# Output projection of a recurrent attention loop: column halves in two PSUM banks, the last three blocks in two passes

## The chip, the cores and the metric

The kernel runs on one core of one Trainium2 chip. The metric is the time of one execution on the device in microseconds (us), lower is better. A profile is one further execution, taken by the hardware profiler.

## The reference

Two independent parts write the two halves of the output's columns. Part B is a state-space convolution over 2048 steps, which the change does not touch. Part A is attention over 64 segments of 32 rows, where 8 memory rows of each segment's result become part of the next one's input:

```python
for s in range(n_seg):                       # 2048 / 32 = 64 segments
    xs = x[:, s * seg_len:(s + 1) * seg_len, :].copy()
    h = jnp.concatenate([mem, xs], axis=1)   # 8 + 32 rows of 1024
    q = jnp.einsum('btd,dhe->bhte', h, Wq)   # 32 heads of 128; k and v likewise
    ...
    scores = jnp.einsum('bhqe,bhke->bhqk', q, k) * scale
    scores = jnp.where(mask[None, None], scores, -1000000000.0)
    p = _softmax(scores, axis=-1)
    o = jnp.einsum('bhqk,bhke->bhqe', p, v)
    o = jnp.einsum('bhte,hed->btd', o, Wo)   # the output projection
    mem = o[:, :M, :].copy()                 # 8 rows go into the next segment
    outs.append(o[:, M:, :])
```

So segment s + 1 cannot start its projections before the first rows of segment s's output projection are known.

## The kernel before

Part B runs first; while it runs, the work of part A that doesn't depend on the memory is done (keys, queries and values of the last 8 rows of each segment, "left rows", go to DRAM as PKd and VXd). Then `part_a` loops over the 64 segments, with 32 rows (8 memory rows and 24 others) in `hT`. Schedule and order are written out by hand: each engine executes its instructions in the order of the code, and the framework inserts the waits.

*Weights.* The four weight matrices are cut in blocks of 128 x 2048. Most blocks stay in SBUF for the whole loop. Thirteen blocks a segment are streamed from DRAM (512 KB each) through five slots (`wst`) on SP's queue, in the order of use: k 2 and 3, q 2, k 1 and 5, q 4, v 2 and 7, v 4 and 7, and blocks 4, 8 and 13 of the output projection. A load is issued when the block five places ahead in that order has been used. Block 7 of q and k and block 15 of the output projection are held in PSUM and copied into SBUF when they are due, by DVE: `fetch` (L337), for block 15 two copies into the arena (`Oa`, `Ob`) and one into `S`.

*One segment.* The projections (`quads`, L416) multiply hT, 32 columns wide, with a block in four matmuls of 512 columns that run side by side in four column tiles of TensorE. Then come transposes (L427), scores (L441, L444), the softmax on DVE and ACT, and the value products (`pv_x`, L497 and L501) for two groups of 16 heads, with results o0 and o1 in SBUF. `pv_l` is the value product of the left rows.

*The output projection* (`oproj`, L529) goes through 16 blocks of two heads each. For each head, four matmuls of 256 columns in four column tiles add into a 128 x 256 area of one PSUM bank, `pp[:, 1, :]`: column tile qt holds result columns 256 qt to 256 qt + 255. The blocks run 0 to 4 (from o0), then the second value product, then 5 to 7, then 8, 10, 12, 14, 9, 11, 13, 15 (from o1).

*The end of a segment*, in TensorE's order: `pv_l`; two transposes (L631) of the two 128-column halves of the result; the next segment's first `quads`. Between them: DVE copies the first half of `pp[:, 1, :]` into SBUF (L625), ACT the second (L625), and after the transposes DVE copies the memory rows of each into `hT` (L633):

```python
for j in range(2):
    (nc.scalar.copy if j else nc.vector.tensor_copy)(out=osb[:, 128 * j:128 * j + 128], in_=pp[:, 1, 128 * j:128 * j + 128])
pl = ps.tile([128, 4, 32], F32, name="pl", tag="b2")
pv_l(pl[:], 1, V1, L1)
```

Behind that ACT copies the left rows' results (L636, L639), issues the load of the next PKd and the store to RSd. PSUM banks are named by tags: `b0` to `b3` are used in turn, `keep0` to `keep3` hold the kept blocks. Before the change, both value products are in `b1`, `pp` (the left rows of the first group beside the projection's result) is in `b3`, `pl` in `b2`, and the transposes go to `b0` and `b1`.

After the loop the left rows' output projection runs (L669).

Of the kernel before, what the change touches and what calls it, by code (L numbers as in the profile page):

```python
# [10 lines left out]
BF16 = mybir.dt.bfloat16  # L11
F32 = mybir.dt.float32
# [252 lines left out]
def load_resident(tc, pool, src, key, W_res, eng=None, t_=None):  # L265
    if t_ is None:
        t_ = pool.tile([128, 2048], BF16, name="W_%s" % "_".join(str(i) for i in key))
    (eng or tc.nc.sync).dma_start(out=t_[:].rearrange("e (h d) -> e h d", h=2) if key[0] == "o" else t_[:], in_=src(key))
    W_res[key] = t_


def part_a(ctx, tc, x, src, WD, HE, seg_len, out_a, ahead, W_res, rest, places, first):
    nc = tc.nc
    S, Dm = x.shape
    M = 8
    SL = seg_len
    E = 128
    KC = Dm // 128
    NS = S // SL
    assert SL == 32 and M == 8 and Dm == 1024 and HE == 4096  # L280
    XM = 24
# [5 lines left out]
    ident, mask, BD, BDx, BDL, hT = ahead.consts  # L287
# [14 lines left out]
    def unit(key):  # L302
        if key in rest:

            rest.remove(key)
            load_resident(tc, wres, src, key, W_res, None, places.pop(0)() if places else None)
        if key in W_res:
            return W_res[key]
        if key in KEPT:
            return ahead_of.pop(key) + halves.get(key, [])  # L310
        between.pop(key, lambda: None)()
        if key in first:
            return first.pop(key)
        if key[0] == "v":
            for k_ in rest[0:3 if key[1] == 0 else 1]:
                rest.remove(k_)
                load_resident(tc, wres, src, k_, W_res, None, outs.pop(0) if outs else None)
        return stage(key, WD[key][:])
# [3 lines left out]
    ps = ctx_l.enter_context(tc.tile_pool(name="a_ps", bufs=1, space=PSUM))  # L322
# [16 lines left out]
    def stage(key, in_):  # L339
        t_ = wst.tile([128, 2048], BF16, name="wst", tag="w%d" % (loads[0] % SLOTS))  # L340
        loads[0] += 1
        nc.sync.dma_start(out=t_[:].rearrange("e (h d) -> e h d", h=2) if len(in_.shape) == 3 else t_[:], in_=in_)
        return t_
# [26 lines left out]
    def columns(w, lo, n):  # L370

        if not isinstance(w, list):
            return [(0, w[:, lo:lo + n])]
        return [(max(lo, l_) - lo, t_[:, max(lo, l_) - l_:min(lo + n, l_ + n_) - l_]) for l_, n_, t_ in w if l_ < lo + n and lo < l_ + n_]

    def load_pk(j):
        pk = at("pk", 512)
        nc.scalar.dma_start(out=pk, in_=PKd[j])
        return pk
# [28 lines left out]
    for s in range(NS):  # L408
        def quads(m, t, kcs, a=None):
            if a is None:  # L410
                a = ps.tile([128, 512], F32, name="acc", tag=BANK[m, t])
            for kc in kcs:
                w = unit((m, t, kc))
                for g in range(4):
                    for o_, rhs in columns(w, 512 * g, 512):
                        nc.tensor.matmul(a[32 * g:32 * g + 32, o_:o_ + rhs.shape[1]], lhsT=hT[:, kc, :], rhs=rhs,  # L416
                                         start=(kc == 0), stop=(kc == KC - 1), tile_position=(0, 32 * g), skip_group_check=True)
            return a

        def evac(a, name):  # L420
            q = at(name, 512)
            nc.scalar.copy(out=q, in_=a[:])  # L422
            return q
# [35 lines left out]
        def powers(sc, i):  # L459
            nc.scalar.activation(out=flat(sc, i), in_=flat(sc, i), func=ACT.Exp, scale=scale)  # L460

        def weigh(sc, i, pn):
            x, m_ = flat(sc, i), maxima(i)
            nc.vector.tensor_reduce(out=m_, in_=x, axis=AX.X, op=ALU.add)  # L464
            nc.vector.reciprocal(out=m_, in_=m_)
            pn = at(pn, x.shape[1], NK)
            nc.vector.tensor_tensor(out=pn, in0=x, in1=bc(m_.unsqueeze(2), [128, x.shape[1], NK]), op=ALU.mult)
            return pn

        def turn(pn, pt):  # L470
            n = pn.shape[1]
            pt = at(pt, n + n // 4, SL)
            nc.vector.transpose(out=pt[:, 0:n, :], in_=pn[:, :, 0:SL])
            nc.vector.transpose(out=pt[:, n:n + n // 4, :], in_=pn[:, :, SL:NK])  # L474
            return pt
# [19 lines left out]
        def pv(p, t, V, pb, lbs):  # L495
            for hl in range(4):
                nc.tensor.matmul(p[:, hl, :], lhsT=V[:, 128 * hl:128 * hl + 128], rhs=pb[:, hl, :],  # L497
                                 start=(hl == 0), stop=False, skip_group_check=True)
            p, lo = p.rearrange("p a b -> p (a b)"), 0
            for lb in lbs:  # L500
                nc.tensor.matmul(p[:, lo:lo + lb.shape[1]], lhsT=vl[:, t, :], rhs=lb,  # L501
                                 start=False, stop=True, skip_group_check=True)
                lo += lb.shape[1]

        def pv_x(t, V, pb, lbs):

            p = ps.tile([128, 4, 128], F32, name="pv", tag="b1")
            pv(p[:], t, V, pb.rearrange("p a b c -> p a (b c)"), lbs)
            return p

        def evac_o(p, name, parts=1):
            o, n = at(name, 4, 4, SL), 4 // parts
            for i in range(0, 4, n):
                copy = nc.vector.tensor_copy if i + n < 4 else nc.scalar.copy
                copy(out=o[:, i:i + n], in_=p[:, i:i + n, :].rearrange("p a (g q) -> p a g q", g=4))
            return o

        def pv_l(pl, t, V, L):

            pv(pl, t, V, L[:, 0].rearrange("p (a b) k -> p a (b k)", a=4), [L[:, 1].rearrange("p a k -> p (a k)")])  # L520

        def oproj(po, us, oT):
            for u in us:
                w = unit(("o", u))
                for hh in range(2):
                    h = 2 * u + hh
                    for qt in range(4):
                        for o_, rhs in columns(w, 1024 * hh + 256 * qt, 256):
                            nc.tensor.matmul(po[32 * qt:32 * qt + 32, o_:o_ + rhs.shape[1]], lhsT=oT[:, h % 4, (h % 16) // 4, :], rhs=rhs,  # L529
                                             start=False, stop=(h == 31), tile_position=(0, 32 * qt), skip_group_check=True)  # L530

        a = quads("k", 0, (0, 2, 4, 6, 1, 3, 5, 7))
        k0 = evac(a, "k0")
# [2 lines left out]
        a = quads("q", 0, range(0, 6))  # L536
# [4 lines left out]
        a = quads("k", 1, range(0, 3))  # L541
# [16 lines left out]
        a = quads("q", 1, range(KC))  # L558
# [3 lines left out]
        a = quads("v", 0, range(0, 4))  # L562
# [34 lines left out]
        a = quads("v", 1, range(0, 5))  # L597
        vl = vx[:, 0:256].rearrange("p (t e) -> p t e", t=2)
        pv0 = pv_x(0, V0, pb0, lb0)
        pp = ps.tile([128, 2, 256], F32, name="pp", tag="b3")  # L600
        pv_l(pp[:, 0, 0:128].rearrange("p (a k) -> p a k", a=4), 0, V0, L0)
        o0 = evac_o(pv0, "o0")
# [6 lines left out]
        V1 = evac(a, "V1")  # L609
        if s + 1 < NS:  # L610
            put_xt(vx)
        below(sc1, 1)
        powers(sc1, 1)
        oproj(pp[:, 1, :], range(0, 5), o0)
        pv1 = pv_x(1, V1, pb1, [lb1])
        o1 = evac_o(pv1, "o1", 2)
        lt1 = turn(weigh(sc1, 1, "ln1"), "lt1")
        oproj(pp[:, 1, :], range(5, 8), o0)
        L1 = left_blocks(lt1, 0, "L1")
        fetch(("o", 15))  # L620
        oproj(pp[:, 1, :], (8, 10, 12, 14, 9, 11, 13, 15), o1)
        ob = at("ob", 2, 256)
        osb = ob[:, 0, :]
        for j in range(2):
            (nc.scalar.copy if j else nc.vector.tensor_copy)(out=osb[:, 128 * j:128 * j + 128], in_=pp[:, 1, 128 * j:128 * j + 128])  # L625
        pl = ps.tile([128, 4, 32], F32, name="pl", tag="b2")
        pv_l(pl[:], 1, V1, L1)
        if s + 1 < NS:
            pt_o = [ps.tile([128, 4, SL], BF16, name="tro", tag=tag) for tag in ("b0", "b1")]
            for j in range(2):  # L630
                nc.tensor.transpose(out=pt_o[j][:].rearrange("p a b -> p (a b)"), in_=osb[:, 128 * j:128 * j + 128], identity=ident[:])  # L631
            for j in range(2):
                nc.vector.tensor_copy(out=hT[:, :, XM:SL].rearrange("p (q j) r -> p j q r", j=2)[:, j], in_=pt_o[j][:, :, XM:SL])  # L633
        if s + 1 < NS:
            fetch(("k", 0, 7))
        nc.scalar.copy(out=ob[:, 1, 0:128], in_=pp[:, 0, 0:128])  # L636
        if s + 1 < NS:
            pk = load_pk(s + 1)
        nc.scalar.copy(out=ob[:, 1, 128:256], in_=pl[:].rearrange("p a k -> p (a k)"))  # L639
        if s + 1 < NS:  # L640
            stores(s, ob)

# [1 line left out]
    wo = {}  # L644
# [17 lines left out]
    for b in range(4):  # L662
        pe = [ps_k.tile([128, 512], F32, name="pe", tag="keep%d" % (2 * (b % 2) + n)) for n in range(2)]
        for u in order:
            for hh in range(2):
                h = 2 * u + hh
                hi = 16 * (h // 16) + 4 * (h % 4) + (h % 16) // 4
                for n in range(2):
                    nc.tensor.matmul(pe[n][:], lhsT=left[2 * b + hi // 16][:, 128 * (hi % 16):128 * (hi % 16) + 128],  # L669
                                     rhs=wo[u][:, 1024 * hh + 512 * n:1024 * hh + 512 * n + 512], start=(u == order[0] and hh == 0),  # L670
                                     stop=(u == order[-1] and hh == 1))
# [1120 lines left out]
```

## Time and profile before

| | |
|---|---|
| Runs | 1873.58, 1884.78, 1887.85 us; median 1884.78 |
| Profiled execution | 1869.79 us, span 1868.1 us, mean granted clock 0.982 |
| Loop of part A | about 640 to 1840 us of the span |
| TensorE (PE) | 1763.2 us busy, 94% of the span, 31563 matmuls |
| VectorE (DVE) | 1344.2 us, 72% |
| ScalarE (ACT) | 924.7 us, 50% |
| Output projection (L529), all 64 segments | groups of 108.6, 92.8 us and smaller ones |
| DMA | 627.78 MB, mean 336 GB/s |

How to read it: a matmul's time in the profile is from its start to its modelled end, and matmuls overlap, so that counts and starts say more than busy times. PE stands for matmuls, PEld for weight loads, POOL for GpSimd, SP for the queue that issues the weight loads. In a row of the timeline the columns are start, length of the whole group, engine, line, operation, output and input tile, shape, count and, in brackets, the idle time before it with what ended it. The DMA share is the mean busy share of the core's 16 DMA engines.

### The profile page before, as it was taken

The page shows a single profiled execution, that of the slowest core. Times are in us where ns is not written, and L with a number is a line of the kernel's source. Part 1 is how long each engine was busy: PE and PEld are TensorE (multiplying, and loading weights), DVE is VectorE, ACT ScalarE, POOL GpSimd, SP SyncE. Part 2 cuts the span into 40 slices and gives each one's busy share as a digit, 9 for nine tenths or more (in the row PEclk, how much of TensorE's full clock was granted, in tenths as well). Part 3 has the DMA queues.
Part 4 walks back from the last instruction along what each step waited for, and adds up shares of the span by engine and source line. Part 5 has one row for each costly group of instructions (what it writes and reads, how often), then busy time and mean ns, then how long its engine had stood idle before and what let it go on. Part 6 is the DMA issues. An engine that isn't in the chain of part 4 may idle for free.

```text
span 1868.1 us, 73881 instructions
## 1 busy us (share of the span) xinstructions
PE 1763.2 (94%) x31563; PEld 1083.0 (58%) x31563; DVE 1344.2 (72%) x3367; ACT 924.7 (50%) x1663; POOL 518.9 (28%) x908
## 2 busy tenths in 40 slices
PE   8999999877986999999999999999999999999999
PEld 3666665556773655555555555555655555555554
DVE  8599989889992666676767676666766676767650
ACT  8799999881112444444444444444443444444430
POOL 2355454437871111111111111111111111211130
PEclk8999999989997999999999999999999999999999
DMA  8889999678889999999999999999999999999993
GB/s 225 248 247 265 269 264 272 194 217 283 265 299 366 375 391 376 378 380 384 385 390 388 384 389 387 377 381 388 389 384 384 371 387 380 384 383 378 383 367 87
DMA packets 350961, 627.78 MB, mean 336 GB/s; under 512 B 95124, under 2 KB 217500, under 8 KB 348584
## 3 DMA queue, kind: packets, MB, share of 16 engines
q1 hardware_dynamic: 307160, 568.55, 85.3%
q10 hardware_dynamic: 36816, 29.59, 4.8%
q0 software_dynamic: 6656, 24.92, 3.6%
q8 instruction: 247, 4.05, 0.9%
q14 instruction: 82, 0.67, 0.1%
HBM read 565.48 MB, written 72.16 MB: 341 GB/s over the span
## 4 chain that ended last, share of the span: by engine, by line
PE 64%; DVE 14%; DMA 12%; ACT 4%; issue 3%; POOL 2%; SPq 0%; DVEq 0%; POOLq 0%; ACTq 0%
PE acc L416 31%; PE pp L529 13%; PE tr L427 3%; PE pe L669 3%; DMA wst<-WD_v 3%; DMA wq<-Ud 2%; PE pv L497 2%; PE pro L184 2%; DMA wst<-WD_q 2%; PE pv L501 2%; DVE nr L1278 2%; DMA arena<-VXd 1%; PE pro L197 1%; DVE gr L1244 1%; PE ptt L1256 1%
## 5 line engine op out<-in xcount | busy, mean ns | idle before, releaser
L416 PEld LDWEIGHTS <-a_hT 128*32 128x32 bf16 x12351 | 323.0, 96 | 290.8 <-issue 28.4
L422 ACT CAST arena<-acc 128x512 bf16<-128x512 f32 x384 | 224.8, 585 | 376.9 <-PE acc L416 308.9
L416 PE MATMUL acc<-wst,a_hT 128*32 128x512 bf16 x2564 | 255.8, 381 | 9.5 <-DMA wst<-WD_v 6.7
L529 PEld LDWEIGHTS <-arena 128*32 128x32 bf16 x8256 | 216.4, 96 | 65.9 <-issue 40.6
L430 POOL COPY arena<-arena 128x128 bf16<-128x128 bf16 x128 | 37.4, 292 | 675.3 <-PE tr L427 336.4
L337 DVE TENSOR_SCALAR arena<-keep 128x256 int32<-128x256 int32 x508 | 174.3, 395 | 24.2 <-PE acc L416 24.2
L416 PE MATMUL acc<-XM,a_hT 128*32 128x512 bf16 x2560 | 185.2, 380 | 0.4 <-issue 0.4
L197 PE MATMUL pro<-XM,wsl 128*128 128x512 bf16 x512 | 122.6, 383 | 3.6 <-DVE kst L206 2.2
L460 ACT ACTIVATE sc<-sc 128x160 f32<-128x160 f32 (+1 forms) x192 | 63.9, 333 | 120.6 <-DVE sc L457 120.5
L456 DVE TENSOR_REDUCE a_mx<-sc 128x4 f32<-128x160 f32 (+1 forms) x192 | 71.9, 374 | 70.4 <-PE sc L444 70.3
L416 PE MATMUL acc<-W,a_hT 128*32 128x512 bf16 x1280 | 118.3, 387 | 1.1 <-issue 1.1
L546 DVE COPY arena<-tr 128x512 bf16<-128x512 bf16 x64 | 27.2, 425 | 124.9 <-PE tr L427 124.9
L464 DVE TENSOR_REDUCE a_mx<-sc 128x4 f32<-128x160 f32 (+1 forms) x192 | 73.0, 380 | 55.7 <-ACT sc L460 55.2
L491 POOL TENSOR_TENSOR arena<-arena,a_BD 128x128 bf16<-128x128 bf16 x128 | 51.0, 399 | 216.4 <-DVE arena L474 208.5
L529 PE MATMUL pp<-W_o,arena 128*32 128x256 bf16 x3072 | 108.6, 273 | 1.0 <-issue 0.8
L416 PE MATMUL acc<-W_q,a_hT 128*32 128x512 bf16 x1536 | 108.2, 379 | 0.3 <-issue 0.3
L1278 DVE TENSOR_SCALAR nr<-ptt 128x456 f32<-128x456 int16 x128 | 80.4, 628 | 29.2 <-PE ptt L1256 26.3
L1270 ACT ACTIVATE E<-pa 128x648 bf16<-128x648 f32 x128 | 87.9, 712 | 14.9 <-PE pa L1262 13.1
L529 PE MATMUL pp<-W,arena 128*32 128x256 bf16 x2560 | 92.8, 274 | 0.0
L625 ACT CAST arena<-pp 128x128 bf16<-128x128 f32 x64 | 17.0, 265 | 148.8 <-DVE arena L625 148.8
L416 PE MATMUL acc<-g,a_hT 128*32 128x512 bf16 x1024 | 90.4, 380 | 0.0
L416 PE MATMUL acc<-wq,a_hT 128*32 128x512 bf16 x1024 | 90.0, 382 | 0.4 <-issue 0.4
(342 smaller groups left out, 3972.9 us busy)
## 6 DMA issues: line engine op xcount, KB each, us to landing
wst<-WD_k SPq DMA_DIRECT2D x256, 512.0 KB
wst<-WD_v SPq DMA_DIRECT2D x256, 512.0 KB
wst<-WD_o SPq DMA_DIRECT2D x192, 512.0 KB
wst<-WD_q SPq DMA_DIRECT2D x128, 512.0 KB
Ud<-ux POOLq DMA_DIRECT2D x16, 1024.0 KB, 7.6
wq<-Ud SPq DMA_DIRECT2D x32, 512.0 KB
wsl<-in_A_Wk_dram SPq DMA_DIRECT2D x16, 512.0 KB
wsl<-in_A_Wv_dram SPq DMA_DIRECT2D x16, 512.0 KB
```

The costliest lines, as they stand in the source:

```text
L197: nc.tensor.matmul(a[:], lhsT=w[:, kc, 128 * j:128 * j + 128], rhs=xTl[:, kc, :, :].rearrange("p s k -> p (s k)"), start=(kc == 0), stop=( ...
L337: nc.vector.tensor_scalar(out=out.bitcast(I32), in0=in_.bitcast(I32), scalar1=0, scalar2=None, op0=ALU.bitwise_or)
L416: nc.tensor.matmul(a[32 * g:32 * g + 32, o_:o_ + rhs.shape[1]], lhsT=hT[:, kc, :], rhs=rhs, start=(kc == 0), stop=(kc == KC - 1), tile_pos ...
L422: nc.scalar.copy(out=q, in_=a[:])
L427: nc.tensor.transpose(out=p[:, hl, :, :].rearrange("p a b -> p (a b)"), in_=q[:, 128 * hl:128 * hl + 128], identity=ident[:])
L456: nc.vector.tensor_reduce(out=m_, in_=x, axis=AX.X, op=ALU.max)
L460: nc.scalar.activation(out=flat(sc, i), in_=flat(sc, i), func=ACT.Exp, scale=scale)
L464: nc.vector.tensor_reduce(out=m_, in_=x, axis=AX.X, op=ALU.add)
L529: nc.tensor.matmul(po[32 * qt:32 * qt + 32, o_:o_ + rhs.shape[1]], lhsT=oT[:, h % 4, (h % 16) // 4, :], rhs=rhs, start=False, stop=(h == 3 ...
L669: nc.tensor.matmul(pe[n][:], lhsT=left[2 * b + hi // 16][:, 128 * (hi % 16):128 * (hi % 16) + 128], rhs=wo[u][:, 1024 * hh + 512 * n:1024 ...
L1270: sc.activation(out=T["E", r, e // 4][:, lo:lo + 8 * NE].rearrange("p (i c) -> p i c", i=2), in_=T.pop(("p", r, e))[:, :, 0:4 * NE], func= ...
L1278: v.tensor_scalar(out=T["n", r, e // 4][:, lo:lo + 8 * NT], in0=T.pop(("t", r, e))[:, 0:8 * NT].bitcast(I16)[:, 0:16 * NT:2], scalar1=floa ...
```

## The change

The projection's result is kept as two 128-column halves in two banks: the first halves where they were, the second halves in a new tile `po` in `b1`. Every head therefore takes eight matmuls of 128 columns, four into each bank. Blocks 11, 13 and 15 run all their first halves, then all their second halves. Both copies of the result are ACT's. The first transpose comes ahead of `pv_l`, the second behind it, into the spare columns of `pl`'s bank. The second value product moves from `b1` to `b2`, since `po` is in `b1` from the start of the projection.

```diff
         def pv_x(t, V, pb, lbs):
-            p = ps.tile([128, 4, 128], F32, name="pv", tag="b1")
+            p = ps.tile([128, 4, 128], F32, name="pv", tag=("b1", "b2")[t])
...
-        def oproj(po, us, oT):
+        def oproj(us, oT, js=(0, 1)):
             for u in us:
-                w = unit(("o", u))
-                for hh in range(2):
-                    h = 2 * u + hh
-                    for qt in range(4):
-                        for o_, rhs in columns(w, 1024 * hh + 256 * qt, 256):
-                            nc.tensor.matmul(po[32 * qt:32 * qt + 32, o_:o_ + rhs.shape[1]], lhsT=oT[:, h % 4, (h % 16) // 4, :], rhs=rhs,
-                                             start=False, stop=(h == 31), tile_position=(0, 32 * qt), skip_group_check=True)
+                if u not in wo:
+                    wo[u] = unit(("o", u))
+                for h in (2 * u, 2 * u + 1):
+                    for j in js:
+                        for qt in range(4):
+                            for o_, rhs in columns(wo[u], 1024 * (h - 2 * u) + 256 * qt + 128 * j, 128):
+                                nc.tensor.matmul(po[j][32 * qt:32 * qt + 32, o_:o_ + rhs.shape[1]], lhsT=oT[:, h % 4, (h % 16) // 4, :], rhs=rhs,
+                                                 start=(j == 1 and h == 0), stop=(h == 31), tile_position=(0, 32 * qt), skip_group_check=True)
...
+        po, wo = (pp[:, 1, 0:128], ps.tile([128, 128], F32, name="po", tag="b1")[:]), {}
-        oproj(pp[:, 1, :], range(0, 5), o0)
+        oproj(range(0, 5), o0)
...
-        oproj(pp[:, 1, :], (8, 10, 12, 14, 9, 11, 13, 15), o1)
+        oproj((8, 10, 12, 14, 9), o1)
+        for j in range(2):
+            oproj((11, 13, 15), o1, (j,))
...
-            (nc.scalar.copy if j else nc.vector.tensor_copy)(out=osb[:, 128 * j:128 * j + 128], in_=pp[:, 1, 128 * j:128 * j + 128])
-        pl = ps.tile([128, 4, 32], F32, name="pl", tag="b2")
-        pv_l(pl[:], 1, V1, L1)
+            nc.scalar.copy(out=osb[:, 128 * j:128 * j + 128], in_=po[j])
+        pl = ps.tile([128, 192], F32, name="pl", tag="b2")
         if s + 1 < NS:
-            pt_o = [ps.tile([128, 4, SL], BF16, name="tro", tag=tag) for tag in ("b0", "b1")]
-            for j in range(2):
-                nc.tensor.transpose(out=pt_o[j][:]..., in_=osb[:, 128 * j:128 * j + 128], identity=ident[:])
+            pt_o = [ps.tile([128, 4, SL], BF16, name="tro", tag="b0")[:]..., pl[:, 128:192].bitcast(BF16)]
+            nc.tensor.transpose(out=pt_o[0], in_=osb[:, 0:128], identity=ident[:])
+        pv_l(pl[:, 0:128].rearrange("p (a k) -> p a k", a=4), 1, V1, L1)
+        if s + 1 < NS:
+            nc.tensor.transpose(out=pt_o[1], in_=osb[:, 128:256], identity=ident[:])
```

More of the change, by code (lines that the diff above doesn't have):

```diff
@@ L617, in part_a @@
         lt1 = turn(weigh(sc1, 1, "ln1"), "lt1")
-        oproj(pp[:, 1, :], range(5, 8), o0)
+        oproj(range(5, 8), o0)
         L1 = left_blocks(lt1, 0, "L1")
         fetch(("o", 15))
-        oproj(pp[:, 1, :], (8, 10, 12, 14, 9, 11, 13, 15), o1)
+        oproj((8, 10, 12, 14, 9), o1)
+        for j in range(2):
+            oproj((11, 13, 15), o1, (j,))
         ob = at("ob", 2, 256)
@@ L624, in part_a @@
         for j in range(2):
-            (nc.scalar.copy if j else nc.vector.tensor_copy)(out=osb[:, 128 * j:128 * j + 128], in_=pp[:, 1, 128 * j:128 * j + 128])
-        pl = ps.tile([128, 4, 32], F32, name="pl", tag="b2")
-        pv_l(pl[:], 1, V1, L1)
+            nc.scalar.copy(out=osb[:, 128 * j:128 * j + 128], in_=po[j])
+        pl = ps.tile([128, 192], F32, name="pl", tag="b2")
         if s + 1 < NS:
-            pt_o = [ps.tile([128, 4, SL], BF16, name="tro", tag=tag) for tag in ("b0", "b1")]
+            pt_o = [ps.tile([128, 4, SL], BF16, name="tro", tag="b0")[:].rearrange("p a b -> p (a b)"), pl[:, 128:192].bitcast(BF16)]
+            nc.tensor.transpose(out=pt_o[0], in_=osb[:, 0:128], identity=ident[:])
+        pv_l(pl[:, 0:128].rearrange("p (a k) -> p a k", a=4), 1, V1, L1)
+        if s + 1 < NS:
+            nc.tensor.transpose(out=pt_o[1], in_=osb[:, 128:256], identity=ident[:])
             for j in range(2):
-                nc.tensor.transpose(out=pt_o[j][:].rearrange("p a b -> p (a b)"), in_=osb[:, 128 * j:128 * j + 128], identity=ident[:])
-            for j in range(2):
-                nc.vector.tensor_copy(out=hT[:, :, XM:SL].rearrange("p (q j) r -> p j q r", j=2)[:, j], in_=pt_o[j][:, :, XM:SL])
+                nc.vector.tensor_copy(out=hT[:, :, XM:SL].rearrange("p (q j) r -> p j q r", j=2)[:, j],
+                                      in_=pt_o[j].rearrange("p (a b) -> p a b", a=4)[:, :, XM:SL])
         if s + 1 < NS:
@@ L638, in part_a @@
             pk = load_pk(s + 1)
-        nc.scalar.copy(out=ob[:, 1, 128:256], in_=pl[:].rearrange("p a k -> p (a k)"))
+        nc.scalar.copy(out=ob[:, 1, 128:256], in_=pl[:, 0:128])
         if s + 1 < NS:
```

## The prediction

> **What bounds the kernel now.** I read the page first, then the busy time by stretch, then who waited for whom, the chain of waits and the timeline of one segment's end.
>
> ```profile
> span 1868.1 us, 73881 instructions
> ...
> PE 1763.2 (94%) x31563; PEld 1083.0 (58%) x31563; DVE 1344.2 (72%) x3367; ACT 924.7 (50%) x1663; POOL 518.9 (28%) x908
> ...
> q8 instruction: 247, 4.05, 0.9%
> ...
> PE 64%; DVE 14%; DMA 12%; ACT 4%; issue 3%; POOL 2%; SPq 0%; DVEq 0%; POOLq 0%; ACTq 0%
> ```
>
> TensorE alone seems to bound it: 94% busy, 64% of the chain. The changed loop over 64 segments fills about 640 to 1840 us; there the busy time by stretch (columns: length, busy time and count of PE, PEld, DVE, ACT, POOL; granted clock; DMA share; GB/s) says something else:
>
> ```profile
> 700.00:800.00 100.00, 97.53 (x2097) 57.50 (x2085) 68.84 (x216) 43.01 (x94) 17.05 (x43) 1.00 1.00 379
> 900.00:1000.00 100.00, 98.92 (x2150) 58.50 (x2142) 68.22 (x214) 44.03 (x96) 16.78 (x41) 1.00 1.01 389
> ...
> 1400.00:1500.00 100.00, 97.06 (x2118) 57.44 (x2118) 68.86 (x219) 43.08 (x95) 17.46 (x41) 1.00 1.00 379
> 1700.00:1800.00 100.00, 96.16 (x2061) 56.76 (x2060) 67.34 (x212) 42.56 (x93) 19.75 (x46) 1.00 1.01 380
> ```
>
> The DMA share is 1.00 to 1.01 in each stretch: the 16 engines have no free time. Where they moved 389 GB/s, PE was busy 98.9%; where 379 to 380, 96.2 to 97.5%. PE's busy share follows the transfers. Segments by their end (the copy into hT, L633, from the timelines), then all of them:
>
> ```profile
> 670.73 0.47 DVE L633 COPY a_hT<-tro 128x32 bf16<-128x32 bf16 x2 [0.32 <-PE tro L631]
> 689.29 0.47 DVE L633 COPY a_hT<-tro 128x32 bf16<-128x32 bf16 x2 [0.32 <-PE tro L631]
> 707.83 0.47 DVE L633 COPY a_hT<-tro 128x32 bf16<-128x32 bf16 x2 [0.32 <-PE tro L631]
> 727.62 0.47 DVE L633 COPY a_hT<-tro 128x32 bf16<-128x32 bf16 x2 [0.32 <-PE tro L631]
> L633 DVE COPY a_hT<-tro x122: 165/175/176, 652.2 to 1787.4; 128x32 bf16<-128x32 bf16 x122
> ```
>
> Undisturbed segments take 18.56 and 18.54 us, a late one 19.79. The mean is (1787.4 - 652.2 - 0.3)/60 = 18.92 (61 pairs of copies, the second of a pair about 0.3 after the first). So some 0.37 us a segment is lateness. What is late is seen in the chain of waits:
>
> ```profile
> 1407.12 1.50 PE acc L416 x25
> 1408.61 7.29 DMA wst<-WD_v
> ...
> 1415.94 0.61 PE acc L416 x8
> ```
>
> A streamed weight block was 7.29 us under way, from the moment its slot came free to the matmul that needed it. PE's chain and the DMA thus stand within 2% of each other, and the DMA is the one without slack. The table of waits shows little of it (the largest, below, is 2.9 us), because lateness hides in matmuls whose modelled time overlaps.
>
> ```profile
> PE acc L416 <- DMA wst<-WD_v: 2.9, 4, 1.9
> ```
>
> **The change part by part.** The end of an undisturbed segment, from its timeline:
>
> ```profile
> 706.13 0.65 DVE L337 TENSOR_SCALAR arena<-keep 128x256 int32<-128x256 int32 x2
> 706.27 0.49 PE L529 MATMUL pp<-wst,arena 128*32 128x256 bf16 x8
> ...
> 706.60 0.50 PE L529 MATMUL pp<-arena 128*32 128x256 bf16 x4
> ...
> 706.70 0.21 DVE L337 TENSOR_SCALAR a_S<-keep 128x64 int32<-128x64 int32 x1
> 706.97 0.22 PE L529 MATMUL pp<-a_S,arena 128*32 128x128 bf16 x1
> ...
> 707.22 0.29 DVE L625 CAST arena<-pp 128x128 bf16<-128x128 f32 x1 [0.31 <-PE pp L529]
> ...
> 707.54 0.27 ACT L625 CAST arena<-pp 128x128 bf16<-128x128 f32 x1 [2.27 <-DVE arena L625]
> ...
> 707.57 0.53 PE L631 MATMUL tro<-a_ident,arena 128*128 128x128 bf16 x2
> ...
> 707.86 0.10 PEld L631 LDWEIGHTS <-arena 128*128 128x128 bf16 x1 [0.20 <-ACT arena L625]
> ...
> 708.06 0.40 PE L416 MATMUL acc<-Wlow,a_hT 128*32 128x512 bf16 x4
> ```
>
> Two things are to be seen. The copies of the two halves run one after the other though on two engines (ACT waits for DVE's copy of the same bank), and both only after the last matmul: 706.97 to 708.06 is 1.09 us. And that last matmul stands 0.06 after DVE's copy of the kept block 15 into S ends (706.91): here DVE, not PE, sets the end.
>
> *The split matmuls.* 32 heads x 4 = 128 matmuls of 256 columns (one cut in two: 129) become 256 of 128, in groups of four side by side.
>
> ```profile
> 1206.02 2.81 PE acc L416 x52
> ...
> 1214.11 1.09 PE pp L529 x40
> ```
>
> A group of four takes 2.81/13 = 0.216 us at 512 columns and 1.09/10 = 0.109 at 256, so on that line 0.0555 at 128: 0.111 a head instead of 0.109, +0.064 us a segment, of which +0.02 (the ten heads before the second value product) lies ahead of DVE's work. Whether pairs of weight load and matmul can come that fast is bounded by the shortest such matmuls here:
>
> ```profile
> 396.22 0.22 PE L1068 MATMUL kp<-gi 128*32 128x49 bf16 x4
> ...
> 396.98 0.22 PE L1068 MATMUL kp<-gi 128*32 128x49 bf16 x4
> ```
>
> Between these starts lie 22 groups of four, 0.76/22 = 0.0345 us each: 8.6 ns a pair, below the 13.9 needed. The other end is the present 27.3 ns a pair; I take 13.9, as a faster pace is seen.
>
> [...]
>
> *The end in halves, DVE setting it.* The first halves' last matmul needs the second of DVE's two L337 copies (ends 706.78): 706.84. Six groups of second halves (3 blocks x 2 heads) follow: 706.84 + 0.33 = 707.17, by when S is long there. ACT's copy 0 starts 0.25 after its last matmul (as 706.97 to 707.22), 707.09, and ends 707.36; transpose 0 at 707.41, the left rows' value product behind it. Copy 1, on ACT too, starts 707.42, ends 707.69; transpose 1 at 707.74; the next segment 0.20 later (as 707.86 to 708.06), 707.94. The hT copy follows transpose 0 as before by 0.26 and gates at 707.90, so it isn't last. That is 0.12 earlier; less 0.02 gives **0.10 us a segment**. Most of the expected overlap is lost, since the second halves of blocks 11 and 13 now stand behind a first half that waits for DVE.
>
> *The end in halves, PE setting it.* In the segment ending at 1219 DVE was done before PE needed its copy:
>
> ```profile
> 1218.00 0.21 DVE L337 TENSOR_SCALAR a_S<-keep 128x64 int32<-128x64 int32 x1
> ...
> 1218.35 0.22 PE L529 MATMUL pp<-a_S,arena 128*32 128x128 bf16 x1
> ```
>
> There copy 1 starts at once after the last matmul and the next segment follows by 0.25 + 0.27 + 0.05 + 0.20 = 0.77 instead of 1.09: 0.32 less 0.06, so 0.26 us. Over 63 segment ends PE's chain gets shorter by 6.3 to 16.4 us.
>
> *Banks.* The second value product goes to the bank that V1's accumulator leaves, and V1's copy precedes it anyway; the second halves take the bank of the first value product, whose copy to o0 the projection waits for already. Nothing; if that cover were gone, a copy of 512 columns would be waited for, up to four times ACT's 0.27 for 128. DVE loses a copy of 0.29, ACT gains one of 0.27 while idle (2.27 idle ahead of its copy); load_pk and the store behind it shift under 0.1 against the next segment.
>
> *Slots and queues.* No load is added and the order on SP's queue stays. Block 13 is read again in the second pass, so its slot comes free about 0.27 later against DVE's end, 0.39 against the next segment; the load behind it waits on SP, with four others under way.
>
> *Code.* 127 more pairs are 254 instructions a segment.
>
> ```profile
> q8 instruction: 182, 2.98, 1.1%
> ```
>
> That row is for 700 to 1800; over the run 247 packets served 63126 PE instructions, 256 each. So one more packet a segment, 1.1% x 16 x 1100/182 = 1.06 us of one DMA engine, 0.066 us of sixteen; by bytes (16.4 KB at 383 GB/s) 0.043. Over 63 segments **2.7 to 4.2 us** of DMA time where none is free; I take 4.2, since the share counts time. Three such packets a segment (182 in 1100/18.92 = 58 segments) already pass in undisturbed segments without showing, which excludes much more.
>
> *Sum.* DMA pays +4.2. Of PE's 6.3 to 16.4 the loop can use only what the DMA can follow: between nothing (share 1.00) and all. I take 2 us, a third of the DVE-set value, since segments do reach 18.54. Net **+2.2 us**: 1869.8 + 2.2 = 1872.0 for the profiled execution, whose time is its span and 1.7 around it. That execution lies 15 below the median of the runs shown and below the lowest of them, so the spread of one kernel is as large as anything here. Carried to the median 1884.8: **1887 us**.
>
> **Rivals.**
> *A, the transfers hide the gain* (the forecast): 1887, by itself 1874 to 1898. For it: the share of 1.00; against: undisturbed segments run at PE's pace.
> *B, PE's chain counts in full*: -6 (1878.5) to -16 us (1868.4), the nearer end likelier, as DVE set the end at 707. For it: 64% of the chain.
> *C, slower by block 13's slot*: the load behind it lands late by up to 0.39 us a segment, 63 x 0.39 = +25 us (1909); half is 1897. It decides when that load's landing, now early enough in undisturbed segments, has less than 0.39 in hand. Against: the load queues behind others, so its issue is not what it waits for.
> *D, code arrives too late in the burst*: a packet's 128 pairs now last 128 x 13.9 = 1.78 us instead of 3.5. From a request-to-landing time over 1.78 PE starves; each 0.5 us beyond it costs twice that a segment, 63 us (1948). For it: 1.06 us of transfer alone; against: nothing shows how far ahead code is asked for. [...]
> *E, a pace floor*: if 27.3 ns a pair is a floor and not streaming, 127 x 27.3 ns x 63 = +218 us (2103). Against: the 8.6 ns above. [...]
>
> **How the numbers follow.** A 0.56, B 0.25, C 0.12, D 0.05, E 0.02. The likeliest gives 1887. The range 1867 to 1905 takes in B and the nearer half of C. One per cent, 18.8 us, is about what a measurement of this kernel can tell from no change. Faster by more: only the far end of B with the runs' spread, 0.09. Slower by more: D, E, half of C and A's tail, 0.16. Within: 0.75.
>
> **What would show it.** Right: the DMA share still 1.00 to 1.01; some 310 code packets in the run; the next segment's first matmul 0.9 to 1.05 after S is copied, instead of 1.15; undisturbed segments near 18.45 but the mean still about 18.9, with more lateness at streamed blocks. Wrong: a mean under 18.8 (B); the loads after block 13 named in the chain far oftener (C); idle "issue" time inside the projection (D); split matmuls over 14.5 ns apart (E).

## The result and the profile after

| | before | after |
|---|---|---|
| Runs measured side by side | 6, 1873.58 to 1887.85 us | 6, 2117.38 to 2131.59 us |
| Median | 1881.27 us | 2125.88 us |
| Ratio | | 1.1293, 95% interval 1.1262 to 1.1324 |
| Profiled execution | 1869.79 us | 2122.91 us |

The change makes the kernel 245 us slower. The forecast was 1887 us, its range 1867 to 1905, so both are wrong. What happened is rival D, which had a chance of 0.05: code arrives too late in the burst.

The page of the kernel after, the lines that answer to those of before:

```profile
span 2121.2 us, 90202 instructions
...
PE 1822.4 (86%) x39691; PEld 1131.2 (53%) x39691; DVE 1330.8 (63%) x3303; ACT 941.9 (44%) x1727; POOL 519.0 (24%) x908
...
q8 instruction: 311, 5.10, 1.0%
...
PE 64%; issue 13%; DVE 11%; DMA 6%; ACT 4%; POOL 2%; SPq 0%; DVEq 0%; POOLq 0%; ACTq 0%
```

PE has 8128 more matmuls and 64 more code packets, one a segment, as expected. New is "issue" in the chain, 13% where it was 3%: time in which PE waited for nothing that the profile shows. The busy time by stretch over 1000 us of the loop (same columns as in the prediction), first after, then before:

```profile
700.00:1700.00 1000.00, 849.38 (x23172) 509.73 (x23161) 559.32 (x1757) 370.77 (x834) 146.16 (x352) 0.95 0.89 319
```

```profile
700.00:1700.00 1000.00, 977.65 (x21183) 578.19 (x21172) 687.32 (x2167) 432.52 (x951) 174.14 (x422) 1.00 1.01 383
```

Everything runs less, the DMA too: its share falls from 1.01 to 0.89, so transfers no longer set the time. The granted clock falls from 1.00 to 0.95. Who waited for whom (engine, line, what ended the wait: total us, times, longest), PE in the loop of the kernel after:

```profile
PE pp L530 <- issue: 106.0, 55, 4.2
PE po L530 <- issue: 88.5, 50, 3.4
PE acc L416 <- issue: 7.4, 10, 1.2
PE acc L416 <- DMA wst<-WD_v: 3.2, 4, 1.2
```

The same view of the kernel before:

```profile
PE pp L529 <- issue: 3.8, 7, 1.0
...
PE acc L416 <- issue: 2.2, 6, 0.7
```

So 194.5 us of unexplained waits stand in the projection alone, against 3.8 us in before. Their form is seen in the timeline of one segment's end:

```profile
685.17 0.22 PE L530 MATMUL pp<-W_o,arena 128*32 128x128 bf16 x2
687.06 0.23 PE L530 MATMUL pp<-W_o,arena 128*32 128x128 bf16 x2 [1.67 <-issue]
687.07 0.28 PE L530 MATMUL po<-W_o,arena 128*32 128x128 bf16 x4
687.13 0.27 PE L530 MATMUL pp<-wst,arena 128*32 128x128 bf16 x4
...
688.25 0.33 PE L530 MATMUL pp<-W_o,arena 128*32 128x128 bf16 x8
688.36 0.33 PE L530 MATMUL pp<-wst,arena 128*32 128x128 bf16 x8
688.47 0.27 PE L530 MATMUL pp<-Whalf,arena 128*32 128x128 bf16 x4
688.53 0.27 PE L530 MATMUL pp<-arena 128*32 128x128 bf16 x4
688.59 0.33 PE L530 MATMUL po<-W_o,arena 128*32 128x128 bf16 x8
688.70 0.33 PE L530 MATMUL po<-wst,arena 128*32 128x128 bf16 x8
688.81 0.22 PE L530 MATMUL po<-Whalf,arena 128*32 128x128 bf16 x2
690.79 0.23 PE L530 MATMUL po<-Whalf,arena 128*32 128x128 bf16 x2 [1.76 <-issue]
690.80 0.28 PE L530 MATMUL po<-arena 128*32 128x128 bf16 x3
690.86 0.22 PE L530 MATMUL po<-a_S,arena 128*32 128x128 bf16 x1
```

PE stops in the middle of a group of four, once after two of it in a resident block (685.17) and once after two of it in `Whalf` (688.81): no weight, no bank and no other engine changes there. Between the two resumptions at 687.06 and 690.79 lie 2 + 4 + 80 (20 groups from 687.13 to 688.20) + 8 + 8 + 4 + 4 + 8 + 8 + 2 = 128 matmuls, with their weight loads 256 instructions: one code packet (79382 of them for 311 packets in this run, 255 each). They take 1.78 us and then PE is idle for the rest of 3.73 us. The DMA queues in narrow stretches (packets that start there, MB, share of 16 engines) show a code packet from 684.8 to 685.0 us and the next from 688.1 to 688.3, none between:

```profile
q8 instruction: 1, 0.02, 27.4%
...
q8 instruction: 1, 0.02, 31.7%
```

By these shares of 0.2 us x 16 engines, the packets last 0.88 and 1.01 us. So the second starts 1.04 to 1.24 us after PE resumed, lasts 1.01, and PE goes on 1.5 to 1.7 us after its end. These three parts make the 3.73 us; only 1.78 of it is covered by work.

The rest of the trace bears this out. In all 115 waits for "issue" of over 0.3 us in this loop, PE goes on 1.12 to 1.62 us after the end of the latest code packet. Wherever two of them stand under 200 matmuls apart, 52 times, 128 matmuls lie between (43 times) or 127 (9 times).

The waits of PE for "issue" in the loop, with three rows of 1.4 to 2.7 us at the value products, are 208 us; before had 6.8 (with one row of 0.8). That is 201 of the 253 us between the two profiled executions. With a long stall there can come a second loss: for 40 of the 69 waits of PE of 1.5 us or more in this loop a stretch with a granted clock of 0.50 begins inside the wait or up to 1.81 us behind it, and for no shorter wait. The timeline at 1214 us, and the busy time of the stretch behind it:

```profile
1213.59 0.27 PE L530 MATMUL pp<-arena 128*32 128x128 bf16 x1 [3.49 <-issue]
...
1215.47 0.64 PE L416 MATMUL acc<-wst,a_hT 128*32 128x512 bf16 x4
1215.90 0.64 PE L416 MATMUL acc<-Wlow,a_hT 128*32 128x512 bf16 x4
...
1219.10 0.38 PE L416 MATMUL acc<-wst,a_hT 128*32 128x512 bf16 x4
1219.32 0.60 PE L416 MATMUL acc<-W_q,a_hT 128*32 128x512 bf16 x8
```

```profile
1215.00:1218.40 3.40, 3.40 (x34) 1.27 (x37) 1.56 (x6) 0.27 (x1) 0.00 (x0) 0.50 0.89 280
```

Around the 3.49 us without code the granted clock is 0.50, from 1212.05 to 1218.88 us, and groups of four at 512 columns start 0.43 us apart instead of 0.22. The clock fell 1.95 us into that wait, which began at 1210.10; it was also 0.50 from 665.92 to 669.33, behind a wait of 1.72 us that ended at 665.92. The remaining 253 - 201 = 52 us of the loss fit this, as the clock of the loop is 0.50 for 140 of its 1455 us (never in before), which is at most 70 us lost, but no run separates them.

### The profile page after: what moved, and what is told of

Its sections match the earlier page's. It is cut to its first block, busy times and chain, and to the rows that moved or that the text cites. A ratio compares the mean times of both kernels' runs of the same rounds, so it can differ in the third digit from the quotient of the medians.

```text
span 2121.2 us, 90202 instructions
## 1 busy us (share of the span) xinstructions
PE 1822.4 (86%) x39691; PEld 1131.2 (53%) x39691; DVE 1330.8 (63%) x3303; ACT 941.9 (44%) x1727; POOL 519.0 (24%) x908
## 4 chain that ended last, share of the span: by engine, by line
PE 64%; issue 13%; DVE 11%; DMA 6%; ACT 4%; POOL 2%; SPq 0%; DVEq 0%; POOLq 0%; ACTq 0%
PE acc L416 32%; PE pp L530 7%; PE po L530 6%; PE tr L427 3%; PE pe L675 3%; DMA wst<-WD_v 2%; PE pv L497 2%; PE pro L184 2%; DMA wq<-Ud 2%; PE pv L501 1%; DVE nr L1284 1%; PE pro L197 1%; PE ptt L1262 1%; POOL Bt L1505 1%; PE ups L1042 1%
## 5 line engine op out<-in xcount | busy, mean ns | idle before, releaser
L416 PEld LDWEIGHTS <-a_hT 128*32 128x32 bf16 x12351 | 328.5, 99 | 328.9 <-issue 78.6
L530 PEld LDWEIGHTS <-arena 128*32 128x32 bf16 x16384 | 256.2, 101 | 249.7 <-issue 234.7
L416 PE MATMUL acc<-wst,a_hT 128*32 128x512 bf16 x2564 | 272.1, 399 | 7.9 <-DMA wst<-WD_v 7.2
L416 PE MATMUL acc<-XM,a_hT 128*32 128x512 bf16 x2560 | 185.0, 380 | 1.0 <-issue 0.8
L530 PE MATMUL po<-W_o,arena 128*32 128x128 bf16 x3072 | 126.7, 233 | 49.4 <-issue 49.4
L530 PE MATMUL pp<-W_o,arena 128*32 128x128 bf16 x3072 | 115.7, 232 | 55.8 <-issue 55.8
L638 DVE COPY a_hT<-tro 128x32 bf16<-128x32 bf16 x63 | 11.0, 175 | 218.3 <-PE tro L633 218.3
L416 PE MATMUL acc<-W,a_hT 128*32 128x512 bf16 x1280 | 119.6, 386 | 0.0
L416 PE MATMUL acc<-W_q,a_hT 128*32 128x512 bf16 x1536 | 113.1, 387 | 3.1 <-issue 3.0
L530 PE MATMUL pp<-W,arena 128*32 128x128 bf16 x2560 | 90.4, 220 | 12.3 <-issue 12.3
L416 PE MATMUL acc<-Wlow,a_hT 128*32 128x512 bf16 x768 | 93.8, 469 | 4.2 <-issue 4.2
```

The costliest lines, as they stand in the source:

```text
L530: nc.tensor.matmul(po[j][32 * qt:32 * qt + 32, o_:o_ + rhs.shape[1]], lhsT=oT[:, h % 4, (h % 16) // 4, :], rhs=rhs, start=(j == 1 and h == ...
```

## The experiments

Each experiment ran on the same chip as runs of the kernel before beside it: 1881.28 us (median) beside e1 to e4, 1877.31 (one run) beside e5 to e8, 1883.38 beside e9 to e12. e5 to e8 and e12 are single runs. "Pairs" are a weight load with its matmul. In the expectations, theory S is that code is supplied more slowly than PE uses it, and theory T that the new end of the segment (banks, copies, transposes) is what costs. One matmul of block 15 was cut at 128 columns already, so the full split adds 127 pairs and not 128, e8 63, and the split of blocks 11, 13 and 15 adds 23 where the expectations say 24.

### The number of pairs, their place, and the new end

**e2, the split alone.** The kernel before with every 256-column matmul of the projection cut in two, in one bank, with the old end.

```diff
                     for qt in range(4):
-                        for o_, rhs in columns(w, 1024 * hh + 256 * qt, 256):
-                            nc.tensor.matmul(po[32 * qt:32 * qt + 32, o_:o_ + rhs.shape[1]], ...)
+                        pass
+                    n = 128 if True else 256
+                    for c in range(0, 256, n):
+                        for qt in range(4):
+                            for o_, rhs in columns(w, 1024 * hh + 256 * qt + c, n):
+                                nc.tensor.matmul(po[32 * qt:32 * qt + 32, c + o_:c + o_ + rhs.shape[1]], ...)
```

> The kernel before, with nothing changed but each projection matmul of 256 columns cut into two of 128, in the one bank. Theory S: as the changed kernel or a little more, 2100 to 2150 us, with idle 'issue' time of 2 to 4 us at a time in the projection. Theory T: 1880 to 1892.

Measured 2143.59 us, ratio 1.1402 (1.1363 to 1.1440). The waits of PE:

```profile
PE pp L533 <- issue: 192.2, 99, 3.7
```

The split by itself brings the whole loss and the same stalls. Banks, copies and transposes of the change are not needed for it.

**e1, the change without the split of the other 13 blocks.** The blocks other than 11, 13 and 15 run in 256-column matmuls; the new end stays.

```diff
                 for h in (2 * u, 2 * u + 1):
+                    if len(js) == 2:
+                        for qt in range(4):
+                            for o_, rhs in columns(wo[u], 1024 * (h - 2 * u) + 256 * qt, 256):
+                                nc.tensor.matmul(pp[32 * qt:32 * qt + 32, 1, o_:o_ + rhs.shape[1]], ..., start=False, stop=False, ...)
+                        continue
                     for j in js:
...
-                                                 start=(j == 1 and h == 0), stop=(h == 31), ...)
+                                                 start=(j == 1 and h == 22), stop=(h == 31), ...)
```

> The changed kernel, but blocks 0 to 10, 12 and 14 (all but 11, 13, 15) in matmuls of 256 columns into pp alone, so that the second halves of the output lack these 13 blocks; two banks, two passes for the last three blocks, both copies on ACT, transposes and value products as in the changed kernel. Theory S (code supply: TensorE uses a packet of 128 pairs of weight load and matmul faster than the next one comes, 1.8 us against some 3.7): the projection has 152 pairs instead of 256, as long-lasting as before, so 1870 to 1895 us, idle 'issue' time at the projection under 1 us a segment. Theory T (the new end of the segment, banks or copies, is what costs): 2100 or more, as the changed kernel.

Measured 1929.58 us, ratio 1.0268 (1.0240 to 1.0297). Four fifths of the loss are gone with 104 of the 127 added pairs, but the 23 that stay still cost 48 us. That was more than expected.

**e3, as many pairs elsewhere.** The projection as before; five of the eight blocks in each set of `quads` are cut from four matmuls of 512 columns into eight of 256, 120 pairs a segment.

```diff
+                n = 256 if kc in (1, 2, 3, 4, 6) else 512
+                for c in range(0, 512, n):
                     for g in range(4):
-                    for o_, rhs in columns(w, 512 * g, 512):
+                        for o_, rhs in columns(w, 512 * g + c, n):
...
```

> The kernel before, with the projection whole and 120 more pairs a segment put elsewhere: in the query, key and value projections the blocks 1, 2, 3, 4 and 6 run in eight matmuls of 256 columns instead of four of 512. Nearly the same amount of code as the changed kernel (some 305 packets), but 128 pairs there last 4.3 us on the average of five split and three whole blocks. Theory S: 1880 to 1900 us, hardly slower. Theory A (the amount of code, through DMA time or issue): 2100 or more.

Measured 2066.64 us, ratio 1.1003 (1.0967 to 1.1039). I had expected little here, since 128 pairs of five split and three whole blocks last 4.3 us, longer than the 32 groups x 0.109 = 3.5 us of the projection of before, which hardly stalls. The waits:

```profile
PE acc L418 <- issue: 112.4, 92, 2.7
PE pp L531 <- issue: 19.8, 28, 1.5
```

So 4.3 us for a packet, on the average, is too fast as well when several packets in a row go at that pace; before's projection has one packet's worth at 3.5, between stretches at 0.216 us a group. What counts here is the rate over more than one packet, not the width of 128 columns.

**e4, the end alone, slower.** One DVE copy of 256 columns takes the place of the two copies.

```diff
-        for j in range(2):
-            (nc.scalar.copy if j else nc.vector.tensor_copy)(out=osb[:, 128 * j:128 * j + 128], in_=pp[:, 1, 128 * j:128 * j + 128])
+        nc.vector.tensor_copy(out=osb, in_=pp[:, 1, :])
```

> The kernel before, with both halves of the result copied by one DVE copy of 256 columns (0.42 us by a like copy) instead of DVE's and then ACT's of 128 (0.59 from start to end): PE's chain gets some 0.1 us a segment shorter, with no code added. If the DMA hides PE's gains, as the prediction had it: within 3 us of before. If PE's chain counts in full: 6 to 8 us faster.

Measured 1885.29 us, ratio 1.0019 (0.9995 to 1.0042). One segment's end in its timeline:

```profile
716.07 0.22 PE L529 MATMUL pp<-a_S,arena 128*32 128x128 bf16 x1
716.37 0.42 DVE L624 CAST arena<-pp 128x256 bf16<-128x256 f32 x1 [0.94 <-PE pp L529]
...
717.35 0.40 PE L416 MATMUL acc<-Wlow,a_hT 128*32 128x512 bf16 x4 [0.21 <-DVE a_hT L632]
```

The end takes 1.28 us here and took 1.09: it got longer, not shorter as expected, since the next segment now waits for the copy into hT. Over all 63 ends the mean is 1.24 against 1.11, 63 x 0.13 = 8 us on PE's chain; the time shows 4 (-1 to 8). So e4 does not decide whether the time pays for PE's chain in full.

### Is the DMA's load part of it?

e5 is the changed kernel and e6 the kernel before, with every streamed weight block replaced by one that lies in SBUF; e7 splits blocks 0 to 7 only, e8 blocks 8 to 15 only, both with the old end.

```diff
-        return stage(key, WD[key][:])
+        return W_res[("o", 0) if key[0] == "o" else ("k", 0, 0)]
```

> The changed kernel without the thirteen streamed loads a segment: a resident block is used in their place (wrong weights, same instructions on TensorE). The DMA engines are nearly idle in the loop. If code comes late because its packets queue behind the weight loads (theory S1): stalls in the projection mostly gone, 1830 to 1880 us. If asking for a packet has a fixed delay of some 3 us whatever the load (theory S2): stalls as before the cut, 2050 us or more.

> The kernel before without the streamed loads, in the same way. Late weight loads are gone, so the loop runs at PE's pace: 63 x 0.37 us less, 1840 to 1850 us, mean segment 18.5 to 18.6 us. Little changed (1865 or more) would mean that the lateness was not the weight loads'.

Measured 1905.61 us for e5 and 1849.49 for e6. The stretch of 1000 us of e5, then its waits:

```profile
700.00:1700.00 1000.00, 947.75 (x27361) 588.70 (x27354) 657.31 (x2070) 437.71 (x982) 171.07 (x415) 1.00 0.08 23
```

```profile
PE pp L530 <- issue: 26.9, 31, 2.6
PE po L530 <- issue: 23.7, 31, 1.4
```

With the DMA at 0.08 the same code costs 56 us instead of 245, and the stalls shrink from 194.5 to 50.6 us. That lies between what the two theories of the expectation gave. So code packets are late for two reasons: PE uses them faster than a nearly idle DMA brings them, and 189 of the 245 us come only with the weight streams. e6 says that the streams cost the kernel before 28 us.

```diff
+                    n = 128 if u < 8 else 256      # e8: u >= 8
+                    for c in range(0, 256, n):
```

> The kernel before, with only blocks 0 to 7 of the projection in matmuls of 128 columns (64 more pairs a segment, in the first half of the projection). Theory S: the stalls come once what is fetched ahead is used up; the 192 pairs of the projection last 3.5 us where code for them takes 5 to 6, so 1 to 2 us a segment, 1945 to 2010 us. Theory T: 1880 to 1890.

> The same with only blocks 8 to 15 split (64 more pairs, in the last half, 128 pairs in 1.8 us right ahead of the segment's end). Theory S: 1 to 2 us a segment, 1945 to 2010 us, the stalls in the last blocks. Theory T: 1880 to 1890.

Measured 2023.05 us (e7) and 2044.21 (e8): +146 and +167 us for 64 and 63 pairs a segment, more than expected and more than half of e2's 262. Neither place is the cause by itself. A part of e8's stalls has moved behind the projection, 25.0 us at L416 where before had 2.2:

```profile
PE pp L533 <- issue: 84.5, 48, 3.6
PE acc L416 <- issue: 25.0, 21, 2.8
```

### Few pairs, and fewer streams

**e9, only blocks 11, 13 and 15 split**, in one bank, with the old end: e1 without the new end.

```diff
+                    n = 128 if u in (11, 13, 15) else 256
+                    for c in range(0, 256, n):
```

> The kernel before, with only blocks 11, 13 and 15 in matmuls of 128 columns, in one bank and in one pass: the 24 more pairs of the first-thirteen-whole kernel without its new end. Supply theory, put as a rate (some 3.2 us for every code packet beyond the 193 that the loop before takes): 12 packets more, 1920 to 1935 us, the same as the first-thirteen-whole kernel. If that kernel's 48 us were its new end's (banks, copies, passes): 1880 to 1892.

Measured 1909.02 to 1945.14 us in four runs (median 1925.84, without the slowest 1923.41), ratio 1.0190 (1.0114 to 1.0265), beside e1's 1.0268 (1.0240 to 1.0297). With the same pairs, old and new end cannot be told apart.

**e10 and e11, 24 pairs out elsewhere.** In e1 and in the kernel before, the 16 score matmuls (L441) of a group become four of 160 columns.

```diff
-            for hl in range(4):
-                for g in range(4):
-                    nc.tensor.matmul(sc[32 * g:32 * g + SL, 0, hl, :], lhsT=QT[:, hl, g, :], rhs=KT[:, hl, g, :], ...)
+            for g in range(4):
+                nc.tensor.matmul(sc[32 * g:32 * g + SL, 0, :, :], lhsT=QT[:, 0, g, :], rhs=KT[:, :, g, :], ...)
```

> The first-thirteen-whole kernel with 24 pairs taken out elsewhere: the sixteen score matmuls of 40 columns become four of 160 that use the first head's queries for all (both groups), so that its code is as long as before's. It shows what the new end of the segment is worth without its code. Supply theory: back to 1870 to 1890 us. New end costly: 1915 or more. If the new end's shorter chain counted in full: 1865 to 1875.

> The kernel before with the same 24 pairs taken out (scores with the first head's queries for all): 377 pairs a segment instead of 401. Supply theory: before has only some 9 us of code stalls in the loop, so 0 to 10 us faster, 1871 to 1881; it is the right partner for the merged first-thirteen kernel. If time followed the amount of code also below before's: 1840.

Measured 1902.45 us for e10, ratio 1.0111 (1.0047 to 1.0176), and 1869.85 for e11, 0.9931 (0.9905 to 0.9957). The waits of e10:

```profile
PE acc L416 <- DMA wst<-WD_v: 13.0, 18, 3.9
PE po L535 <- issue: 9.7, 10, 1.3
PE acc L416 <- issue: 4.8, 9, 0.8
```

e10 has as much code as the kernel before (247 packets) and is still 19 us slower than before, outside the expected range: 23 pairs more in the burst are not made good by 24 fewer elsewhere. Beside e11, its partner, it is 32.6 us slower, 22 ns for each of the 23 pairs. It also waits more for weights. e11 gains 13.5 us; part of it may be the shorter scores themselves, which no run separates.

**e12, ten streams instead of thirteen.** The changed kernel with value blocks 2 and 7 of the first group and 4 of the second taken from SBUF.

```diff
+        if key in (("v", 0, 2), ("v", 0, 7), ("v", 1, 4)):
+            return W_res["k", 0, 0]
         return stage(key, WD[key][:])
```

> The changed kernel with ten streamed blocks a segment instead of thirteen (three value blocks replaced by a resident one: wrong weights, same TensorE code), so that the DMA is some 20% less busy. If code packets are late because they queue behind weight loads, the stalls lie between those of the changed kernel (3.4 us a segment) and those without streams (1.0): 1960 to 2060 us. If the delay only vanishes when the DMA is idle: 2090 or more.

Measured 2047.98 us. The stretch of 1000 us:

```profile
700.00:1700.00 1000.00, 879.04 (x24500) 530.35 (x24492) 588.47 (x1857) 390.60 (x881) 154.51 (x370) 0.97 0.77 264
```

At a DMA share of 0.77 most of the loss stays. Spare DMA time over a whole segment does not bring code in time; most of the loss goes somewhere between ten streams and none, where nothing was measured.

### What a pair costs

Time added, by 64 segments and the pairs added in each:

| | added us | pairs a segment | ns a pair |
|---|---|---|---|
| after | 244.6 | 127 | 30 |
| e2 | 262.3 | 127 | 32 |
| e3 | 185.4 | 120 | 24 |
| e7, e8 | 145.7, 166.9 | 64, 63 | 36, 41 |
| e1, e9 | 48.3, 40.0 | 23 | 33, 27 |
| e5 against e6 | 56.1 | 127 | 7 |

With the streams each added pair costs 24 to 41 ns, though no column of work was added. 3.73 us for 128 pairs, the supply seen at 687 to 691, is 29 ns a pair. So the added pairs are paid for at about the rate at which code arrives.

## Why the prediction was wrong, step by step

*Right: the pace of the split matmuls.* 20 groups from 687.13 to 688.25 take 1.12 us, 0.056 each, as against 0.0555; rival E, a floor of 27.3 ns a pair, is out: in these column tiles the matmuls start 0.056/4 = 14 ns apart.

*Right: the end, where PE sets it.* The next segment was to follow S's matmul (L530 here) by 0.77 us instead of 1.09:

```profile
690.86 0.22 PE L530 MATMUL po<-a_S,arena 128*32 128x128 bf16 x1
691.02 0.23 PE L633 MATMUL tro<-a_ident,arena 128*128 128x128 bf16 x1
...
691.63 0.40 PE L416 MATMUL acc<-Wlow,a_hT 128*32 128x512 bf16 x4
```

It follows by 0.77; the median of all 63 ends is 0.80, before's is 1.10. In the whole kernel it brings 18 us at best (2125.9 against e2's 2143.6, which were not measured side by side), and nothing that can be seen in e1 against e9.

*Right: the number of packets*, 311 where some 310 were named, and their bytes: 1.0% of the engines.

*Wrong: what a packet costs.* The failed step is the paragraph "Code". It priced the added packets by the DMA time that they take, 2.7 to 4.2 us, where 245 were measured, and closed with "Three such packets a segment (...) already pass in undisturbed segments without showing, which excludes much more". They pass because they are spread: 128 pairs took 18.92/3.13 = 6.0 us on average, and 3.5 in the projection for about one packet. That says nothing of a second one 1.78 us behind the first. The packets' share of busy time, 1.0%, does not show a supply of one packet in 3.73 us.

*Wrong: rival D's chance, 0.05.* Its mechanism and its place are what the trace shows: 128 pairs in 1.78 us, PE idle inside the projection. Its price comes out too: 3.73 - 1.78 = 1.95 us of excess, at the 63 us for each 0.5 that D gave, is 246 us. That this meets the measured 245 so closely is luck: 1.95 is from one stretch, and D knew nothing of the halved clock. D also saw danger only in the burst, where e3 stalls at 4.3 us for a packet. It was held down by "nothing shows how far ahead code is asked for". A bound from rows was to be had: before already had 3.8 us of waits for "issue" in its projection, seven of up to 1.0 us, which no engine and no weight transfer explains, in the stretch where a packet lasts 3.5 us. The nine waits for "issue" of over 0.3 us in before's loop also end 1.37 to 1.60 us after the end of a code packet.

How far ahead code is asked for is not shown by the runs either. The trace of after shows waits that stand 128 pairs apart, 256 instructions, and what one of them cost: 1.76 us at 690.79.

*Not settled: the transfers hide the gain (A).* e6 confirms that late weights cost the kernel before some 28 us, where the prediction had 63 x 0.37 = 23. e4 does not decide whether a shorter chain pays, and e11, 13.5 us faster with the same streams at 385 GB/s instead of 383, speaks against a gain that is hidden in full. In the kernel after, at a share of 0.89, the transfers were no longer the limit. *Rival C*, block 13's slot, has no sign: the largest wait for a streamed block is still that for a value block, 3.2 us in all where before had 2.9, and not one for the loads behind block 13.

*Open.* Why a packet starts 1.05 us or more after PE resumes, and what in the loaded DMA delays it. The traces of after and e5 narrow this down: a packet lasts about as long in both (median 1.03 and 1.07 us), and PE goes on about as long after its end (1.42 and 1.37), but after a wait the next packet starts a median of 1.60 us after PE resumes in after and 1.15 in e5. Whether this later start carries all of the 189 us is not shown. e5 and e12 show that the streams matter, not whether code waits behind their packets on the same engines or for memory.

## What to carry to other kernels

Before cutting matmuls narrower, work out how long PE takes for one packet of its code, in the densest stretch and over two or three packets: here 128 pairs in 6 us passed, in 4.3 us several times in a row they did not, and in 1.78 us they cost 3.7 in the stretch shown. A few unexplained "issue" waits of PE in a stretch of small matmuls, those of over 0.3 us ending 1.37 to 1.60 us after a code packet, were the warning here that added instructions would be paid for at about the rate at which code arrives. Cut only what lies on the path (three blocks instead of sixteen took the loss from 245 to 48 us), and compare it with the gain at the end, which was about 0.3 us a segment.

## What was not expected of the hardware

Code packets are 1% of the DMA's time and set this kernel's pace: in the stretch shown, with the weight streams running, 128 pairs came 3.7 us apart, and even with the DMA 92% free the changed projection waited 50.6 us for code. Around a wait for code of 3.49 us the clock was also halved for 6.8 us, from inside the wait on, so that this stall was paid for twice.
